# Attention with a learned position bias and a feed-forward layer: the short query chunk first, two chunks with f32 exponentials transposed on TensorE, the weights' integer steps through PSUM

## The chip, the cores and the metric

The kernel runs on one core of a Trainium2 chip. The metric is the device time of one execution in microseconds (us); the time of the kernel before is the median of three runs. The engines are named as in the profile: PE is TensorE's matmul stream and PEld its weight loads, DVE is VectorE, ACT is ScalarE, POOL is GpSimd, and SP is SyncE, which issues all DMAs of this kernel.

## The reference, cut to what matters

```python
# q, k, v: (4, 8, 576, 64) f32; w1 (1, 32), b1 (32), w2 (32, 8)
scores = scale * np.matmul(q, k.transpose(0, 1, 3, 2))
x = (np.log1p(np.abs(i - j)) / np.log1p(np.maximum(i, 1.0)))[..., None]
bias = np.maximum(x @ w1 + b1, 0.0) @ w2          # (576, 576, 8), one plane a head
scores = scores + bias.transpose(2, 0, 1)[None]
attn = np.exp(scores - np.max(scores, axis=-1, keepdims=True))
attn = attn / (np.sum(attn, axis=-1, keepdims=True) + 1e-09)
y = np.matmul(attn, v)                            # heads side by side: (2304, 512)
h = np.maximum(y @ w_in, 0.0)                     # w_in (512, 2048) float64
out = (h * h @ w_out).astype(np.float32)          # w_out (2048, 512) float64
```

## The kernel before

**Tiling.** The four batches are taken as two pairs (p = 0, 1). A pair's 576 queries are cut into five chunks: c = 1 to 4 hold 128 queries of both batches, c = 0 holds the last 64 queries of both batches side by side on the 128 partitions. One step is (p, c, head), so there are 80 steps, eight to a chunk. In a step with c = 1 to 4 (a full step) the softmax works on two rows of 576 per partition, one for each batch; in a step of c = 0 (a short step) on one. `ORDER` sets the chunks of p = 0 to 3, 0, 2, 4, 1 and those of p = 1 to 1, 0, 4, 2, 3.

**A step.** `qk` multiplies q and k, both split into a high and a low f16 part, into the PSUM tile `sc` (there is one). `softmax_a` adds the bias tile `bt` and takes the row maximum on DVE (L367), forms the negated maximum (L370), and takes the exponential with its sum on ACT (L373). `softmax_b` splits the exponentials into f16 parts: ACT casts (tile `a`, L118 by way of `cast`), POOL subtracts (L384, L385), and a DMA transposes the two parts to `at` (L387). `pv`, called three steps later (`LAG`), multiplies `at` with the split `v` in 28 f16 matmuls of 64 columns (L411). After a chunk's last head `finish_x` scales the chunk, splits it (`xh`, L448 and L449) and transposes it by DMA to `xt`.

**The feed-forward layer.** A finished chunk gives eight units: `g1` (24 matmuls into `hp`, L465, then ACT, DVE and POOL make the squared and split `g`) and, three units later, `g2` (12 matmuls into `o0` and `o1` for a full chunk, 6 into `o0` for the short one, L488). One unit goes with each step, two when more than ten are waiting (`BACKLOG`).

**Weights.** They arrive as float64 in 32 tiles of 128 x 512 values through the staging tiles `stg` (three, shared with k and v). `WT.split` makes f32 of each by three integer instructions on DVE in the SBUF tile `cv` (L185, L186, L188), casts the high part on ACT (`ENG["wh"]`), scales `cv` in place on ACT (`ENG["wl"]`, POOL for the last tiles) and subtracts on POOL (L203). `W_AT` says how many of the 32 tiles are loaded in each of the first 32 steps; they lie between step 4 and step 30.

**Bias.** For 16 query positions and all heads at once, a group, `hgen` makes four hidden tiles `hg` on DVE (L266) or ACT (L263; the string `HID` has the number on ACT for each pair of groups), and `bias_mm` multiplies them in f32 into `bp` (L293), evacuates `be` (L304) and writes it to a table in DRAM (L308); `bias_ld` reads the step's `bt` back. `bias_due` sets how many of the 36 groups are done after each step; ten are done ahead of step 0.

**Order.** A scheduler places the instructions of each engine by priority and by its own estimate of time, so that engines do not follow the source's order strictly; on each engine the built order is then fixed. The PSUM tiles of `bp` and `hp` share two buffers (`ps_h`).

## Time and profile before

| | us |
|---|---|
| median of three runs | 705.91 (705.66 to 707.59) |
| the profiled execution | 710.13 |
| span of its instructions | 708.4 |
| PE busy | 611.1 |
| DVE busy | 453.9 |
| POOL busy | 385.4 |
| ACT busy | 357.3 |

The span runs from the first instruction to the last; the profiled execution took 1.7 us more than its span. Busy times are unions over the whole span, and the engines work in stages with different limits, so the table alone does not tell which engine sets the time: the stages do, and they are read from the rows further below.

### The profile page before, as it was taken

How to read it: one execution, taken by the hardware profiler on the slowest of the kernel's cores; microseconds unless marked ns; L12 is line 12 of the kernel's file. 1: busy time of each engine (PE TensorE's matmuls, PEld its weight loads, DVE VectorE, ACT ScalarE, POOL GpSimd, SP SyncE). 2: the span in 40 equal slices, each digit the busy share in tenths (PEclk: the TensorE clock that was granted, in tenths of full speed). 3: DMA queues.
4: the chain of work that ended last, by engine and by line, in shares of the span. 5: the costliest groups of instructions: out<-in, count | busy, mean ns of one | idle time of the engine just before them, and what ended most of it. 6: DMA issues, size and time to landing. Idle time of an engine off the chain costs nothing.

```text
span 708.4 us, 15644 instructions
## 1 busy us (share of the span) xinstructions
PE 611.1 (86%) x6056; PEld 377.9 (53%) x6056; DVE 453.9 (64%) x977; ACT 357.3 (50%) x710; POOL 385.4 (54%) x375
## 2 busy tenths in 40 slices
...
GB/s 217 213 239 279 225 235 259 233 258 196 194 240 143 175 227 165 158 185 162 211 237 128 174 168 150 84 143 114 141 153 205 190 156 155 95 131 31 25 7 30
DMA packets 235881, 119.25 MB, mean 168 GB/s; under 512 B 196384, under 2 KB 212768, under 8 KB 235808
## 3 DMA queue, kind: packets, MB, share of 16 engines
...
## 4 chain that ended last, share of the span: by engine, by line
PE 52%; DVE 18%; DMA 14%; issue 6%; ACT 5%; POOL 4%; SPq 0%; DVEq 0%; POOLq 0%; ACTq 0%
PE hp L465 20%; PE o L488 19%; DMA at<-a 7%; PE pv L411 5%; PE sc L352 3%; PE bp L293 3%; DVE hg L266 3%; DVE cv L186 3%; POOL a L385 2%; DVE s L367 2%; DVE cv L188 2%; DVE cv L185 2%; DMA biasd<-be 1%; ACT s L373 1%; ACT a L118 1%
## 5 line engine op out<-in xcount | busy, mean ns | idle before, releaser
L465 PE MATMUL hp<-xt,winH 128*128 128x256 f16 (+1 forms) x1280 | 202.4, 268 | 15.3 <-DVE r L473 14.0
L488 PE MATMUL o<-woutH,g 128*128 128x512 f16 x576 | 184.4, 380 | 0.9 <-ACT o L495 0.9
L373 ACT ACTIVATE s<-s,nm 128x576 f32<-128x576 f32 x144 | 110.5, 768 | 136.6 <-DVE nm L370 136.1
L465 PE MATMUL hp<-xt,winL 128*128 128x256 f16 (+1 forms) x640 | 165.7, 267 | 0.3 <-POOL winL L203 0.3
L385 POOL TENSOR_TENSOR a<-s,a 128x1024 f16<-128x1024 f32 (+1 forms) x80 | 162.6, 2033 | 0.0
L465 PEld LDWEIGHTS <-winH 128*128 128x128 f16 x1280 | 118.7, 100 | 51.3 <-issue 20.1
L367 DVE CUSTOM_DVE_ANT_0 s<-sc,bt 128x576 f32<-128x576 f32 x144 | 103.4, 750 | 45.3 <-PE sc L352 23.3
L488 PEld LDWEIGHTS <-g 128*128 128x128 f16 x864 | 82.8, 98 | 90.4 <-issue 6.7
L473 DVE TENSOR_TENSOR r<-hp,r 128x512 f32<-128x512 f32 (+1 forms) x80 | 50.6, 633 | 117.0 <-ACT r L471 116.6
L475 POOL TENSOR_TENSOR g<-r,g 128x512 f16<-128x512 f32 (+1 forms) x80 | 86.8, 1085 | 66.8 <-DVE g L122 64.4
L411 PEld LDWEIGHTS <-at 128*128 128x128 f16 (+1 forms) x2240 | 80.6, 105 | 71.3 <-DMA at<-a 38.7
L384 POOL TENSOR_TENSOR a<-s,a 128x128 f16<-128x128 f32 (+1 forms) x80 | 37.0, 463 | 146.5 <-ACT a L118 118.5
L411 PE MATMUL pv<-v,at 128*128 128x64 f16 (+1 forms) x2240 | 88.8, 199 | 30.7 <-DMA at<-a 28.9
L118 ACT ACTIVATE a<-s 128x1152 f16<-128x1152 f32 (+1 forms) x80 | 85.1, 1064 | 49.9 <-DMA at<-a 48.9
L488 PE MATMUL o<-woutL,g 128*128 128x512 f16 x288 | 109.4, 380 | 0.0
L471 ACT ACTIVATE r<-hp 128x512 f32<-128x512 f32 (+1 forms) x80 | 43.2, 540 | 64.9 <-PE hp L465 64.3
L266 DVE TENSOR_SCALAR hg<-tab_t,nb 128x352 f32<-128x352 f32 (+17 forms) x102 | 67.1, 708 | 13.1 <-PE bp L293 11.4
L293 PE MATMUL bp<-hg,w2s 128*32 128x288 f32 (+17 forms) x352 | 62.0, 550 | 14.8 <-ACT be L304 10.4
L465 PEld LDWEIGHTS <-winL 128*128 128x128 f16 x640 | 64.0, 100 | 8.2 <-issue 0.8
L352 PE MATMUL sc<-k,q 64*128 64x512 f16 x384 | 57.0, 398 | 0.0
L304 ACT ACTIVATE be<-bp,hcst 128x288 f32<-128x288 f32 (+32 forms) x80 | 34.5, 473 | 20.8 <-PE bp L293 14.4
L122 DVE TENSOR_SCALAR g<-r 128x512 f16<-128x512 f32 (+1 forms) x61 | 40.0, 656 | 2.1
...
## 6 DMA issues: line engine op xcount, KB each, us to landing
...
```

The costliest lines, as they stand in the source:

```text
L118: nc.scalar.activation(out=out, in_=in_, func=AF.Copy, scale=scale)
L266: nc.vector.tensor_scalar(ht, tab_t[:, 0:dlen(G)], scl[:, n:n + 1], nb1, op0=ALU.mult, op1=ALU.max)
L293: nc.tensor.matmul(out=bp[32 * t:32 * t + 32, 0:d1 - d0], lhsT=w2s, rhs=ts_[t][:, d0:d1], start=True, stop=True, tile_position=(0, 32 * t))
L352: nc.tensor.matmul(out=sc[:, 1024 * b:1024 * b + 512], lhsT=qt[r, qz, qs], rhs=kt[r, z, 64 * b:64 * b + 512], start=(n == 0), stop=(n == 2 ...
L367: nc.vector.tensor_tensor_reduce(s[:, 576 * b:576 * b + 576], sc[:, 960 * b:960 * b + 576], bt, inv, -3.0e38, ALU.add, ALU.max, mx[:, b:b ...
L373: nc.scalar.activation(out=sl, in_=sl, func=AF.Exp, bias=nm[:, b:b + 1], accum_out=su[:, h, b:b + 1])
L385: nc.gpsimd.tensor_tensor(av[:, :, 640:1152], ev[:, :, 0:512], av[:, :, 0:512], op=ALU.subtract)
L411: nc.tensor.matmul(out=dst, lhsT=lhsT, rhs=vt[:, vz, 5 * b + blk, :], start=(n == 0), stop=(n == 13), tile_position=(0, 0 if c else 64 * b))
L465: nc.tensor.matmul(out=hp[:, f * T:f * T + T].rearrange("p (b t) -> p b t", b=nb), lhsT=wt[:, k, c0:c0 + 128], rhs=xt[:, 0:nb, z * 4 + k, ...
L473: nc.vector.tensor_tensor(rr, hp[:, 0:2 * T], rr, op=ALU.mult)
L475: nc.gpsimd.tensor_tensor(g[:, 1, 0:2 * T], r[:, 0:2 * T], g[:, 0, 0:2 * T], op=ALU.subtract)
L488: nc.tensor.matmul(out=blk["o"][b], lhsT=g[:, z, c0:c0 + 128], rhs=wt[:, 2 * u + f, :], start=(u == 0 and f == 0 and z == 0 and wt is wout ...
```

## The change

- **Order of the chunks.** p = 0 begins with the short chunk: 0, 3, 2, 4, 1. The order of p = 1 stays.
- **Two chunks in f32** (`NF = 2`: the first two, so c = 0 and c = 3 of p = 0). Their exponentials are not split and not sent through a DMA. In `softmax_b` TensorE transposes them in f32 against an identity (five 128-column transposes in a short step, ten in a full one) into tiles `tp` of the pool `ps_h`, and ACT copies these to `at` (two copies in a short step, three in a full one). `pv` multiplies with the unsplit v in ten f32 matmuls.
- **v of p = 0** lands by DMA directly in the tiles of the pool `vp` (nine now) and is split only in steps 16 to 23.
- **Weights.** The first two integer steps write the PSUM tile `ci`, which takes the buffer of `o1`; the third reads it and writes `cv`. All high parts are cast on ACT, all scalings go to POOL. All 32 tiles are loaded in the first 16 steps.
- **Bias.** Four groups are done ahead of step 0, since the short chunk needs four, and `HID` puts 34 hidden tiles on ACT instead of 42.
- **Buffers.** `qst` and `xh` have one buffer instead of two.

```diff
-    "wh": "AAPAAAAA", "wl": "AAAAAAAP", "qh": "PPPDDP",
+    "wh": "AAAAAAAA", "wl": "PPPPPPPP", "qh": "PPPDDP",
...
-HID = "110033320111212000"
+HID = "221111111111111000"
...
+W_AT = [1, 1, 2, 2, 2, 2, 2, 2, 3, 3, 3, 2, 2, 2, 2, 1] + [0] * 16
+ORDER = [[0, 3, 2, 4, 1], [1, 0, 4, 2, 3]]
+NF = 2
...
-    vp = pool("vp", 8)
+    vp = pool("vp", 9)
-    qst_p = pool("qst", 2)
+    qst_p = pool("qst", 1)
-    xh_p = pool("xh", 2)
+    xh_p = pool("xh", 1)
...
+    f32c = [(0, c) for c in ORDER[0][:NF]]
+    def as_f32(t):
+        return t.rearrange("p a b -> p (a b)").bitcast(F32)
+    def v_split(p, h, st):
+        t = vp.tile([128, 2, 640], F16, tag="v", name="v")
+        cast(zn("vh", p * 8 + h), t[:, 0, :], st, float(2 ** VS))
+        nc.vector.scalar_tensor_tensor(
+            out=t[:, 1, :], in0=st, scalar=float(2 ** VS), in1=t[:, 0, :],
+            op0=ALU.mult, op1=ALU.subtract)
+        nc.gpsimd.memset(t[64:128, 1, :].rearrange("p (b j) -> p b j", b=2)[:, :, 256:320], 0.0)
+        v_t[p, h] = t
...
-            self.st = stg_p.tile([128, 1024], F32, tag="stg", name="stg")
+            if self.which == "v" and self.p == 0:
+                self.st = as_f32(vp.tile([128, 2, 640], F16, tag="v", name="v"))
+                v32[self.h] = self.st
+            else:
+                self.st = stg_p.tile([128, 1024], F32, tag="stg", name="stg")
...
-            ci = cv.bitcast(U32)
+            ci = ps_o.tile([128, 512], F32, tag="o1", name="ci").bitcast(U32)
             nc.vector.tensor_scalar(ci, hi32, 3, 0x3FFFFFFF, op0=ALU.logical_shift_left, op1=ALU.bitwise_and)
             nc.vector.scalar_tensor_tensor(out=ci, in0=lo32, scalar=29, in1=ci,
                                            op0=ALU.logical_shift_right, op1=ALU.bitwise_or)
-            nc.vector.scalar_tensor_tensor(out=ci, in0=hi32, scalar=0xC0000000, in1=ci,
+            nc.vector.scalar_tensor_tensor(out=cv.bitcast(U32), in0=hi32, scalar=0xC0000000, in1=ci,
                                            op0=ALU.bitwise_and, op1=ALU.bitwise_or)
...
     def softmax_b(p, c, h):
+        if (p, c) in f32c:
+            at = as_f32(at_p.tile([128, 20, 128], F16, tag="at", name="at")).rearrange("p (k i) -> p k i", i=128)
+            for b in range(nb):
+                tp = ps_h.tile([128, 512], F32, tag="h", name="tp")
+                for k in range(4):
+                    nc.tensor.transpose(tp[:, 128 * k:128 * k + 128], e[:, S * b + 128 * k:S * b + 128 * k + 128], ident)
+                nc.scalar.activation(out=at[:, 4 * b:4 * b + 4, :], in_=tp.rearrange("p (k i) -> p k i", i=128), func=AF.Copy)
+            tp = ps_h.tile([128, 512], F32, tag="h", name="tp")
+            for b in range(nb):
+                nc.tensor.transpose(tp[0:64, 128 * b:128 * b + 128], e[:, S * b + 512:S * b + 576], ident)
+            nc.scalar.activation(out=at[0:64, 4 * nb:5 * nb, :], in_=tp[0:64, 0:128 * nb].rearrange("p (k i) -> p k i", i=128),
+                                 func=AF.Copy)
+            st_[p, c, h, "t"] = at
+            return
...
     def pv(p, c, h):
+            if f32:
+                for blk in range(5):
+                    r = slice(0, 128 if blk < 4 else 64)
+                    if c:
+                        lhsT = at[r, 4 * b + blk if blk < 4 else 8 + b, :]
+                    else:
+                        lhsT = at[r, blk, 64 * b:64 * b + 64]
+                    nc.tensor.matmul(out=dst, lhsT=lhsT, rhs=vt[r, 5 * b + blk, :], start=(blk == 0), stop=(blk == 4),
+                                     tile_position=(0, 0 if c else 64 * b))
+                continue
...
     def bias_due(t):
-        k = (t + AHEAD) // H + 1
+        if t < 0:
+            return due[0]
+        ahead = min(AHEAD, t + 1)
+        k = (t + ahead) // H + 1
...
+        if NF * H <= t < NF * H + H:
+            v_split(0, t - NF * H, v32.pop(t - NF * H))
```

What this moves in the built program is shown at three places. On ACT, at the end of the first full chunk of the kernel before: `a<-s` is the f16 cast that feeds the transposing DMA, `cv<-cv` the scaling of a weight tile, `be<-bp` the evacuation of the bias.

```order
L373 ACTIVATE s,sum<-s,nm 128x576 x2
L118 ACTIVATE woutH<-cv 128x512
L304 ACTIVATE be<-bp,hcst 128x432
L304 ACTIVATE be<-bp,hcst 128x159
L118 ACTIVATE a<-s 128x2x576
L420 ACTIVATE rd<-sum,eps 128x8
L118 ACTIVATE cv<-cv 128x512
```

In the changed kernel, in steps 9 and 10, which belong to its first full chunk, ACT has this (`at<-tp` copies the transposed exponentials out of PSUM):

```order
L388 ACTIVATE s,sum<-s,nm 128x576
L401 ACTIVATE at<-tp 128x512
L388 ACTIVATE s,sum<-s,nm 128x576
L121 ACTIVATE woutH<-cv 128x512
L401 ACTIVATE at<-tp 128x512
L405 ACTIVATE at<-tp 64x256
L485 ACTIVATE os<-ax 128x1
L278 ACTIVATE hg<-tab_t,sm_t 128x384
```

The cast and the scaling are gone from ACT, and three copies per full step stand there, behind transposes on PE.

On DVE, in the same places of the two programs (the end of the first full chunk before; steps 8 to 10 now), the three integer steps of a weight tile:

```order
L185 TENSOR_SCALAR cv<-stg 128x512
L229 SCALAR_TENSOR_TENSOR q<-qst,q 128x512
L370 TENSOR_SCALAR nm<-mx 128x1
L266 TENSOR_SCALAR hg<-tab_t,nb_131 128x400 x2
L370 TENSOR_SCALAR nm<-mx 128x1
L186 SCALAR_TENSOR_TENSOR cv<-stg,cv 128x512
L185 TENSOR_SCALAR cv<-stg 128x512
L188 SCALAR_TENSOR_TENSOR cv<-stg,cv 128x512
```

```order
L281 TENSOR_SCALAR hg<-tab_t,nb_131 128x400
L200 TENSOR_SCALAR ci<-stg 128x512
L281 TENSOR_SCALAR hg<-tab_t,nb_131 128x400 x2
L385 TENSOR_SCALAR nm<-mx 128x1
L201 SCALAR_TENSOR_TENSOR ci<-stg,ci 128x512
L464 TENSOR_TENSOR x<-pv,rd 128x256
L203 SCALAR_TENSOR_TENSOR cv<-stg,ci 128x512
L481 TENSOR_REDUCE ax<-x 128x1
```

The number of instructions per tile is the same; the second operand and, for two of the three, the output lie in PSUM. All 32 tiles now stand ahead of step 16's maximum; before, 22 did and the last ten stood ahead of step 24's.

On PE, the bias group of 496 columns in the last bias chunk (c = 1, steps 24 to 31 in both programs). Before, each of its four matmuls stands alone among those of `g1` or `pv`:

```order
L465 LDWEIGHTS winL
L465 MATMUL hp<-xt,winL 128x128
L465 LDWEIGHTS winH
L465 MATMUL hp<-xt,winH 128x128
L293 MATMUL bp<-hg,w2s 32x496
```

```order
L452 LDWEIGHTS at
L452 MATMUL pv<-v,at 128x64
L308 MATMUL bp<-hg,w2s 32x496 x3
L506 LDWEIGHTS winH
L506 MATMUL hp<-xt,winH 128x256
```

Three of the four now follow each other directly; the groups of 512, 480 and 464 columns, which were split up before too, have all four together.

## Rows read from the trace of the kernel before

**Rows 1.** The busy time of each engine in us, with its number of instructions, then the granted TensorE clock as a share of 2.4 GHz, the DMA share and GB/s, in six stretches (start:end and length come first; the engines follow as PE, PEld, DVE, ACT, POOL). They are cut where DVE starts the first maximum (L367) of steps 0, 8, 16, 24 and 32.

```profile
0.00:32.40 32.40, 20.96 (x129) 6.37 (x130) 23.87 (x61) 21.22 (x44) 12.10 (x22) 0.96 0.68 204
32.40:90.90 58.50, 27.80 (x277) 12.61 (x277) 49.90 (x92) 43.41 (x86) 37.39 (x34) 0.67 0.96 252
90.90:159.70 68.80, 42.26 (x421) 25.25 (x421) 60.72 (x106) 38.48 (x78) 42.45 (x42) 0.78 1.00 245
159.70:235.60 75.90, 63.18 (x589) 35.07 (x591) 65.59 (x119) 47.64 (x94) 55.36 (x48) 0.87 0.81 192
235.60:301.10 65.50, 61.31 (x645) 33.52 (x641) 44.61 (x103) 36.85 (x77) 33.66 (x34) 1.00 0.85 183
301.10:708.40 407.30, 395.61 (x4003) 265.08 (x4001) 209.25 (x503) 169.69 (x336) 204.47 (x197) 1.00 0.65 134
```

**Rows 2.** The chain of work that ended last, after 525 us: start, length, engine, tile, line, number of instructions.

```profile
526.73 1.45 PE hp L465 x24
528.18 1.29 PE o L488 x6
...
548.81 4.94 DMA xt<-xh
...
625.92 1.63 PE pv L411 x56
627.55 2.62 PE hp L465 x24
630.17 2.59 PE o L488 x12
```

**Rows 3.** Who waited for whom from 90 to 236 us: us in total, times, longest.

```profile
PE sc L340 <- DVE mx L367: 16.0, 3, 7.6
...
ACT woutH L118 <- DVE cv L188: 13.7, 7, 5.4
```

**Rows 4.** Groups of instructions on DVE over the whole span: us busy, mean ns of one, idle time before. L188, L186 and L185 are the integer steps of the 32 weight tiles.

```profile
L188 DVE SCALAR_TENSOR_TENSOR cv<-stg,cv 128x512 uint32<-128x512 uint32 x32 | 34.0, 1068 | 0.4
L186 DVE SCALAR_TENSOR_TENSOR cv<-stg,cv 128x512 uint32<-128x512 uint32 x32 | 31.7, 1000 | 0.3
L185 DVE TENSOR_SCALAR cv<-stg 128x512 uint32<-128x512 uint32 x32 | 22.6, 712 | 5.4 <-DMA stg<-w_in 4.6 <-DMA stg<-w_out 0.9
...
L229 DVE SCALAR_TENSOR_TENSOR q<-qst,q 128x512 f16<-128x512 f32 x20 | 17.0, 852 | 9.0 <-POOL q L120 9.0
...
L146 DVE SCALAR_TENSOR_TENSOR k<-stg,k 128x576 f16<-128x576 f32 x14 | 11.6, 830 | 11.4 <-POOL k L120 11.4
```

**Rows 5.** DVE instructions of single lines over the whole span: number, duration in ns as minimum/median/maximum, first and last start, shapes. L473 reads one operand from PSUM and one from SBUF; L186 and L188 read both from SBUF.

```profile
L186 DVE SCALAR_TENSOR_TENSOR cv<-stg,cv x32: 654/750/2548, 43.3 to 214.1; 128x512 uint32<-128x512 uint32 x32
...
L188 DVE SCALAR_TENSOR_TENSOR cv<-stg,cv x32: 634/692/2619, 45.2 to 216.4; 128x512 uint32<-128x512 uint32 x32
...
L473 DVE TENSOR_TENSOR r<-hp,r x80: 407/691/693, 135.4 to 695.0; 128x512 f32<-128x512 f32 x64, 128x256 f32<-128x256 f32 x16
...
L266 DVE TENSOR_SCALAR hg<-tab_t,nb x102: 420/540/2381, 4.6 to 283.4; 128x368 f32<-128x368 f32 x8, 128x384 f32<-128x384 f32 x8, 128x336 f32<-128x336 f32 x7, 128x352 f32<-128x352 f32 x7
...
L367 DVE CUSTOM_DVE_ANT_0 s<-sc,bt x144: 700/752/759, 32.4 to 621.4; 128x576 f32<-128x576 f32 x144
...
L157 DVE SCALAR_TENSOR_TENSOR v<-stg,v x16: 808/1126/2737, 14.8 to 383.0; 128x640 f16<-128x640 f32 x16
```

**Rows 6.** Groups of instructions on POOL up to 160 us, shapes kept apart, columns as in rows 4.

```profile
L385 POOL TENSOR_TENSOR a<-s,a 128x1024 f16<-128x1024 f32 x8 | 19.1, 2387 | 0.0
L203 POOL TENSOR_TENSOR woutL<-cv,woutH 128x512 f16<-128x512 f32 x10 | 13.1, 1321 | 0.1
```

**Rows 7.** Who waited for whom from 235 to 301 us, columns as in rows 3.

```profile
PE pv L411 <- DMA at<-a: 3.8, 2, 2.0
```

**Rows 8.** The chain in the same stretch, columns as in rows 2.

```profile
242.37 7.05 DMA at<-a
```

**Rows 9.** The chain up to 34 us.

```profile
24.51 4.14 DMA biasd<-be
...
28.74 3.63 DMA bt<-biasd
```

**Rows 10.** Groups on ACT over the whole span, shapes kept apart: the evacuation of 288 columns of bias out of PSUM, and a hidden tile of 544 columns.

```profile
L304 ACT ACTIVATE be<-bp,hcst 128x288 f32<-128x288 f32 x7 | 3.4, 492 | 1.6 <-PE bp L293 1.6
...
L263 ACT ACTIVATE hg<-tab_t,sm_t 128x544 f32<-128x544 f32 x3 | 2.4, 833 | 0.0
```

**Rows 11.** PE in order of time; the profile has two records for an f32 matmul. A bias group of 512 columns whose four matmuls stand together, the first and the last of the four of 496 columns that stand alone, and the score matmuls of a full step.

```profile
224.38 1.94 PE L293 MATMUL bp<-hg,w2s 128*32 128x512 f32 x8
...
269.26 1.02 PE L293 MATMUL bp<-hg,w2s 128*32 128x496 f32 x2
...
273.75 1.02 PE L293 MATMUL bp<-hg,w2s 128*32 128x496 f32 x2
...
276.30 0.33 PE L346 MATMUL sc<-kz,q 128*128 128x128 f16 x3
...
286.70 0.82 PE L352 MATMUL sc<-k,q 64*128 64x512 f16 x6
```

**Rows 12.** Weight loads in order of time: 14 f16 loads of 128 columns, and the two of one f32 matmul with 32 columns.

```profile
253.32 0.50 PEld L411 LDWEIGHTS <-at 128*128 128x128 f16 x14
...
254.04 0.14 PEld L293 LDWEIGHTS bp<-hg,w2s 128*32 128x32 f32 x2
```

More of the change, by code (lines that the diff above doesn't have):

```diff
@@ L106, in tile_attention_moe @@
     eps = const.tile([128, 1], F32, name="eps")
+    ident = const.tile([128, 128], F32, name="ident")
     sc = ps_sc.tile([128, 1536], F32, name="sc")
@@ L152, in split @@
                 k_t[self.p, self.h] = t
-            else:
-                t = vp.tile([128, 2, 640], F16, tag="v", name="v")
-                st = st[:, 0:640]
-                cast(zn("vh", self.p * 8 + self.h), t[:, 0, :], st, float(2 ** VS))
-                nc.vector.scalar_tensor_tensor(
-                    out=t[:, 1, :], in0=st, scalar=float(2 ** VS), in1=t[:, 0, :],
-                    op0=ALU.mult, op1=ALU.subtract)
-                nc.gpsimd.memset(t[64:128, 1, :].rearrange("p (b j) -> p b j", b=2)[:, :, 256:320], 0.0)
-                v_t[self.p, self.h] = t
+            elif self.p:
+                v_split(self.p, self.h, st[:, 0:640])
     class WT:
@@ L255, in hgen @@
                 elif pl == "at":
-                    h2 = at_p.tile([128, 18, 128], F16, tag="at", name="hg").rearrange("p k i -> p (k i)").bitcast(F32)
+                    h2 = at_p.tile([128, 20, 128], F16, tag="at", name="hg").rearrange("p k i -> p (k i)").bitcast(F32)
                 elif pl == "s":
@@ L385, in softmax_b @@
         nc.gpsimd.tensor_tensor(av[:, :, 640:1152], ev[:, :, 0:512], av[:, :, 0:512], op=ALU.subtract)
-        at = at_p.tile([128, 18, 128], F16, tag="at", name="at")
+        at = at_p.tile([128, 20, 128], F16, tag="at", name="at")
         nc.sync.dma_start_transpose(out=at[:, 0:9 * nb, :], in_=a[:, 0:nb * 2 * S])
@@ L394, in pv @@
         at = st_.pop((p, c, h, "t"))
-        vt = v_t[p, h].rearrange("p z (j d) -> p z j d", d=D)
+        f32 = (p, c) in f32c
+        vt = v32[h].rearrange("p (j d) -> p j d", d=D) if f32 else v_t[p, h].rearrange("p z (j d) -> p z j d", d=D)
         if h % 4 == 0:
```

11 lines of the change are left out of this document (6 added, 5 removed).

## The prediction

> **What bounds the kernel now.** I read the stretches first, cut where steps 0, 8, 16, 24 and 32 begin [rows 1]. In the last one, 301.1 to 708.4 us, PE is busy for 395.61 of 407.30 us at a granted clock of 1.00, its 2.4 GHz level, and the chain there is PE, unit after unit: 24 matmuls in 2.62 us, 12 in 2.59 us [rows 2]. That part is PE's own work, and nothing ahead of it can shorten it. So the question is only when step 32 begins, how much of PE's work is done by then, and whether the later part gets new waits.
>
> Ahead of it PE is not the limit: busy 27.80 of 58.50 us, 42.26 of 68.80, 63.18 of 75.90, at mean clocks of 0.67 to 0.87, that is, partly at the 1.2 GHz level. DVE is busy for 49.90, 60.72 and 65.59 us of these stretches, 85 to 88% [rows 1], and others wait for it: PE's scores for the maximum, 16.0 us, ACT's weight casts for the last integer step, 13.7 us [rows 3]. DVE's largest item there is the weights: 34.0 + 31.7 + 22.6 = 88.3 us for 32 tiles, 2.78 us each [rows 4]. Their medians are 0.69 and 0.75 us, but single ones take over 2.5 us [rows 5], about as long as POOL's subtraction of 1024 elements, 2387 ns [rows 6]. An instruction of the same length with one operand in PSUM, L473, has a median of 691 and a maximum of 693 ns: it is never held up [rows 5]. I take it that POOL's subtraction holds up DVE instructions that use SBUF twice.
>
> In the fifth stretch, 235.6 to 301.1 us, the weights are gone and DVE is busy for only 44.61 us [rows 1]. What costs there is transposing DMAs on the chain, one of 7.05 us [rows 8], for which PE waits 3.8 us in all [rows 7], and bias matmuls of which below.
>
> **The change part by part.** The sum is made on the span, 708.4 us. The profiled execution took 710.13 us, 1.7 us more, and is itself 4.2 us above the median of 705.91; I work out the shift of the span and set it against the median.
>
> *PE's work left at step 32* is the same. Counting DVE's `r` instructions of the units in the two built programs gives 19 units ahead of step 32 in both: 8 of the short chunk, 8 of c = 3, and 3 of c = 2. All bias is done soon after in both. So the last stretch stays 407.3 us.
>
> *Start.* Four bias groups stand ahead of step 0, not ten. They need 8 hidden tiles on ACT at 0.83 us (6.7 us) and 12 evacuations near 0.49 us (5.9 us) [rows 10], with a weight cast and key copies between them in ACT's order; then, as now, the write (4.14 us) and the read (3.63 us) of the table [rows 9]. Step 0 then starts at about 29 us instead of 32.4; 27 at best, and no gain at worst.
>
> *Steps 0 to 15.* They took 58.5 + 68.8 = 127.3 us, with DVE busy for 110.6. I change DVE's load by what the built programs count between the same steps. Weights: 22 tiles go, which cost 22 x 0.712 + 43 x 1.034 = 60.1 us, and 31.3 come. At L473's 0.69 us a step, 2.07 a tile, that is 64.8 us. An integer step that writes PSUM is in no row: the lower end is the minimum of the SBUF forms, 0.65 us, the upper end the present 2.78 us a tile. I take L473, which has the same size and one PSUM operand; the gain a tile, 0.71 us, is the hold-ups. Hidden tiles: 51 on DVE instead of 27, 24 x 0.54 = 13.0 us. One more k and one more v cost 0.83 + 1.13 us; one split of `xh` fewer saves 1.6 by the length of a q split, 0.85, twice. Sum: +18 us. Against it stands that POOL has no subtractions of exponentials in these 16 steps, 2.4 us each in a full one, but more weight subtractions of 1.3 us [rows 6]. So hidden tiles and v should be near their medians (0.54 and 1.13 us) rather than held for up to 2.4 us, and the ends of neighbouring DVE instructions overlap; I take 7 us off, between 0 and 12. DVE's load is then 122 us (117 to 129), and at the share of now, 110.6/127.3 = 0.87, the 16 steps take 140 us (134 to 148), 13 more than now. Step 16 starts at 169 us instead of 159.7.
>
> *PE in these steps.* Per full step 28 f16 matmuls of 29 ns go (56 in 1.63 us [rows 2]), and 10 f32 matmuls and 10 transposes come. The rows have f32 matmuls with 32 stationary columns only. By them an f32 matmul has two records and costs 1.9 us/2/512, 1.9 ns a column, where four on different columns of the array share it [rows 11]: 0.12 us for 64 columns. Its loads follow each other by 0.03 us for 32 columns, as do f16 loads of 128 [rows 12]. With 128 f32 columns a load takes between 0.03 and 0.12 us, so a matmul between 0.12 and 0.24 us, a transpose between 0.06 (one record) and 0.24. I take 0.24 and 0.16, 4.0 us a full step (1.8 to 4.8) and some 2 us a short one. In steps 8 to 15 PE then has 8 x (4.0 + 1.0 for the scores [rows 11]), 5 us of bias and about 7 us of half units (1.45 + 1.29 us each [rows 2]): 52 us at 2.4 GHz, against some 84 us of DVE. It lies beside DVE's work. The Trainium skill, "TensorE: Matmul & The Clock Gate", section on weight-path perf modes, says that the fast weight load is not used for f32; that speaks for the upper end of a load, and no row here has an f32 load of 128 columns.
>
> *ACT* loses 28 scalings and 16 casts and gains 40 copies of PSUM, each like an evacuation of bias; it was busy 43.41 of 58.5 us at most and stays below DVE. *POOL* loses 16 subtractions and gains 28 scalings; it stays below too. *SP* loses 16 transposing DMAs. Its `qst` loads, with one buffer, wait for the split of the last q, and bias and score loads queue behind them; a q is used for four steps, so I cost this at nothing; uncovered it would be one q split, 0.85 us, each time.
>
> *Steps 16 to 23.* Now 75.9 us with ten weight tiles and DVE at 65.59. After the change DVE's list there is that of the fifth stretch, 44.61 us, which took 65.5 us. That stretch also lost PE time to bias matmuls that stand alone: a group costs 1.94 us/2 together, but 4 x 1.02 us alone [rows 11]. In the changed order the four stand together or 3 and 1, which spares about 6 us in all over four groups. So I take 60 us for steps 16 to 23 (56 to 66), and 63 us for steps 24 to 31 (60 to 66), where two thirds of the units are full ones and PE is the limit: 8 x (5.2 + 1.0 + 0.8) = 56 us and 8 of bias, less half units.
>
> *Later.* With one `xh` buffer the second transposing DMA of a block waits for the first. It shows where no unit is left, as at 548.81 us, 4.94 us on the chain [rows 2]; +3 us (0 to 5).
>
> *Sum.* 29 + 140 + 60 + 63 = 292 us for the start of step 32, where it was 301.1; 292 + 407.3 + 3 = 702.3 us of span, 6.1 below 708.4. Against the median: 705.9 - 6.1 = 700 us.
>
> **The rivals.** *PE is the limit of steps 8 to 15 (slower).* The transposes wait for ACT, the matmuls for ACT's copies, and the next scores stand behind both in PE's fixed order. If PE stays at 1.2 GHz there, its 52 us become 104 against 84 of DVE, and with 16 matmuls f32 at the same rate in the short steps a few more: +20 to +25, 720 us or more. It decides where the mean clock falls below 52/84 = 0.62. The stretch now with PE busy 48% has 0.67, that with 61% has 0.78 [rows 1], which speaks against it; the waits within PE's order speak for it. The Trainium skill has a rule for this side too, in the same page's "PE-mode transpose": it says that the full clock does not engage for transposes. By that the time would be this rival's; the rows have no transposes on PE, and the trace cannot show it.
>
> *The PSUM form is no faster.* At 2.78 us a tile DVE has 31 x 0.71 = 22 us more, 25 us of time: 724 us. For it speaks only that no row has an integer step on PSUM.
>
> *It comes out even.* Each full f32 step passes exponential, transposes, copies and matmuls through two `ps_h` buffers shared with bias and units. Another 0.8 us a full step that DVE spends waiting gives the gain back: 706 us.
>
> *More is released.* If hidden tiles, v and k fall to their minima (0.42, 0.81 us) and the integer steps to 0.65, DVE has 115 us; at 0.88 that is 130, and steps 16 to 23 at 56: 292 - 14 = 278, 686 us.
>
> **How the numbers follow.** About 0.3%, 2.1 us, is what a measurement of this kernel tells from no change, so faster ends at 703.8 and slower begins at 708.0. Forecast, 692 to 703.8: 0.38. More released, 676 to 692: 0.20. Even, 703.8 to 708: 0.16. PE the limit, 708 to 735: 0.20; the PSUM form, 708 to 726: 0.06. So faster 0.58, same 0.16, slower 0.26. The range of 8 in 10 leaves out the lower third of "more" and half of the two slow ones: 681 to 718.
>
> **What would show it.** Right: L201 and L203 with maxima near 0.7 us; step 0 near 29, step 16 near 169, step 24 near 229, step 32 near 292 us; 407 us from there to the end, and PE above 95% busy in them; DVE the busiest engine up to step 16. Wrong: a granted clock below 0.62 in steps 8 to 15 with PE busy throughout (PE the limit); integer steps above 0.9 us (the PSUM form); DVE's share below 0.8 in steps 8 to 15 with PE or ACT waiting on each other (even); step 16 before 160 us (more released). The sum as a whole is wrong if the stretch after step 32 differs from 407 us by more than 5.

## The result, and the profile after

The changed kernel takes 713.04 us (median of 4 runs, 711.86 to 716.15), the kernel before 705.79; the ratio is 1.0104, 95% interval 1.0068 to 1.0139. It is **slower by 1.0%** where the forecast was 0.8% faster. The time lies inside the stated range, on the other side.

The profiled execution took 713.13 us, its span is 711.2. The stretches of the profile after, cut at the first maximum (L382) of steps 0, 8, 16, 24 and 32, columns as in [rows 1]:

```profile
0.00:34.00 34.00, 11.47 (x78) 2.65 (x78) 15.65 (x39) 14.85 (x30) 11.15 (x21) 1.00 0.77 243
34.00:94.20 60.20, 44.74 (x306) 24.21 (x306) 48.32 (x96) 35.94 (x82) 22.94 (x27) 0.77 0.69 208
94.20:175.00 80.80, 65.71 (x436) 43.73 (x436) 73.47 (x151) 46.99 (x104) 48.32 (x61) 0.77 0.67 198
175.00:231.80 56.80, 53.67 (x572) 32.74 (x572) 45.94 (x99) 41.19 (x85) 31.75 (x34) 1.00 0.78 166
231.80:301.70 69.90, 67.42 (x652) 40.09 (x651) 43.70 (x99) 32.84 (x67) 34.87 (x34) 0.98 0.71 155
301.70:711.20 409.50, 396.18 (x4011) 265.03 (x4009) 210.21 (x502) 170.45 (x337) 203.38 (x197) 1.00 0.65 134
```

| us | before [rows 1] | forecast | after | error |
|---|---|---|---|---|
| start | 32.4 | 29 | 34.0 | +5.0 |
| steps 0 to 15 | 127.3 | 140 | 141.0 | +1.0 |
| steps 16 to 23 | 75.9 | 60 | 56.8 | -3.2 |
| steps 24 to 31 | 65.5 | 63 | 69.9 | +6.9 |
| from step 32 on | 407.3 | 410.3 | 409.5 | -0.8 |
| span | 708.4 | 702.3 | 711.2 | +8.9 |

The forecast of the time was 700 us, so 13 us are missing: 8.9 in this table, and the other 4 are the reference, since the profile before was of an execution 4.2 us above its median and the profile after is at its median.

The weights' integer steps after (number, shortest/median/longest in ns, first and last start), against [rows 4, 5]:

```profile
L200 DVE TENSOR_SCALAR ci<-stg x32: 676/694/717, 12.9 to 169.1; 128x512 uint32<-128x512 uint32 x32
L201 DVE SCALAR_TENSOR_TENSOR ci<-stg,ci x32: 677/695/699, 14.8 to 171.9; 128x512 uint32<-128x512 uint32 x32
L203 DVE SCALAR_TENSOR_TENSOR cv<-stg,ci x32: 670/680/689, 22.0 to 172.7; 128x512 uint32<-128x512 uint32 x32
```

None is held up: 2.07 us a tile, as forecast, for 2.78. DVE's load up to step 16 is 48.32 + 73.47 = 121.8 us (forecast: 122).

**The start.** SP's issues in order of time (start, length, line, number), and then two waits up to 34 us (us, times, longest):

```profile
5.27 1.57 SPq L156 DMA_DIRECT2D v<-vd  x3
...
8.44 3.06 SPq L156 DMA_DIRECT2D v<-vd  x4
...
13.67 1.69 SPq L323 DMA_DIRECT2D biasd<-be  x2
...
24.56 1.33 SPq L323 DMA_DIRECT2D biasd<-be  x3
30.29 1.12 SPq L336 DMA_DIRECT2D bt<-biasd  x2
```

```profile
DVE s L382 <- DMA bt<-biasd: 9.8, 1, 9.8
...
ACT be L319 <- DMA biasd<-be: 4.9, 3, 4.1
```

The first bias was evacuated by 11.2 us and its write is issued at 13.67, behind eight loads of v (the first of them at 2.18 us) and two of q at 12.03. ACT then waits 4.9 us for `be` buffers whose writes have not landed. The last write and the read that step 0 waits for take from 24.56 to 34.0 us, against 7.8 us for the two DMAs of [rows 9].

**Steps 24 to 31.** The units' matmuls with `winH` there (number, shortest/median/longest in ns; all are 256 columns wide, so there are full units only), then the chain (start, length):

```profile
L506 PE MATMUL hp<-xt,winH x130: 272/273/421, 234.1 to 301.6; 128*128 128x256 f16 x130
```

```profile
275.81 4.10 DMA xt<-xh
...
279.96 4.41 PE hp L506 x24
```

PE stands still for 2.5 us until the second transposing DMA of the block lands, and the unit behind it takes 4.41 us where [rows 2] have 2.62. The granted clock falls behind the stand: it is 0.74 from 280 to 282 us and 0.51 from 282 to 284.4 us.

### The profile page after: what moved, and what is told of

Its sections match the earlier page's. It is cut to its first block, busy times and chain, and to the rows that moved or that the text cites. A ratio compares the mean times of both kernels' runs of the same rounds, so it can differ in the third digit from the quotient of the medians.

```text
span 711.2 us, 15582 instructions
## 1 busy us (share of the span) xinstructions
PE 639.2 (90%) x6048; PEld 408.5 (57%) x6048; DVE 437.3 (61%) x981; ACT 342.3 (48%) x702; POOL 352.4 (50%) x369
## 4 chain that ended last, share of the span: by engine, by line
PE 48%; DVE 12%; DMA 8%; issue 5%; POOL 3%; ACT 3%; SPq 0%; ACTq 0%; POOLq 0%; DVEq 0%
PE hp L506 18%; PE o L529 18%; DMA at<-a 6%; PE pv L452 4%; PE sc L367 3%; DVE s L382 2%; DVE hg L281 2%; DMA xt<-xh 2%; PE bp L308 2%; POOL a L415 1%; DVE r L514 1%; ACT a L121 1%; DVE xh L490 1%; DVE xh L489 1%; PE sc L355 1%
## 5 line engine op out<-in xcount | busy, mean ns | idle before, releaser
L506 PE MATMUL hp<-xt,winH 128*128 128x256 f16 (+1 forms) x1280 | 198.7, 265 | 3.5 <-DMA xt<-xh 3.1
L382 DVE CUSTOM_DVE_ANT_0 s<-sc,bt 128x576 f32<-128x576 f32 x144 | 103.5, 750 | 52.9 <-PE sc L367 28.0
L415 POOL TENSOR_TENSOR a<-s,a 128x1024 f16<-128x1024 f32 (+1 forms) x64 | 130.4, 2037 | 0.0
L516 POOL TENSOR_TENSOR g<-r,g 128x512 f16<-128x512 f32 (+1 forms) x80 | 85.3, 1066 | 73.4 <-DVE g L125 70.5
L414 POOL TENSOR_TENSOR a<-s,a 128x128 f16<-128x128 f32 (+1 forms) x64 | 28.4, 443 | 133.7 <-ACT a L121 117.7
L121 ACT ACTIVATE a<-s 128x1152 f16<-128x1152 f32 (+1 forms) x64 | 70.4, 1101 | 43.0 <-DMA at<-a 42.2
L281 DVE TENSOR_SCALAR hg<-tab_t,nb 128x464 f32<-128x464 f32 (+17 forms) x110 | 68.1, 673 | 10.2 <-PE bp L308 9.9
L452 PEld LDWEIGHTS <-at 128*128 128x128 f16 (+1 forms) x1792 | 60.3, 100 | 23.6 <-issue 8.1
L452 PE MATMUL pv<-v,at 128*128 128x64 f16 (+1 forms) x1792 | 64.2, 194 | 3.5 <-DMA at<-a 3.5
L308 PE MATMUL bp<-hg,w2s 128*32 128x288 f32 (+17 forms) x352 | 50.1, 574 | 13.2 <-ACT be L319 6.6
L367 PE MATMUL sc<-k,q 64*128 64x512 f16 x384 | 55.1, 395 | 0.0
L445 PEld LDWEIGHTS pv<-v,at 128*64 128x64 f32 (+3 forms) x320 | 40.8, 201 | 20.6 <-issue 11.7
L123 POOL TENSOR_SCALAR cv<-cv 128x512 f32<-128x512 f32 x32 | 21.4, 668 | 55.7 <-ACT winH L121 34.5
```

Source lines behind the costliest of these rows:

```text
L121: nc.scalar.activation(out=out, in_=in_, func=AF.Copy, scale=scale)
L281: nc.vector.tensor_scalar(ht, tab_t[:, 0:dlen(G)], scl[:, n:n + 1], nb1, op0=ALU.mult, op1=ALU.max)
L308: nc.tensor.matmul(out=bp[32 * t:32 * t + 32, 0:d1 - d0], lhsT=w2s, rhs=ts_[t][:, d0:d1], start=True, stop=True, tile_position=(0, 32 * t))
L367: nc.tensor.matmul(out=sc[:, 1024 * b:1024 * b + 512], lhsT=qt[r, qz, qs], rhs=kt[r, z, 64 * b:64 * b + 512], start=(n == 0), stop=(n == 2 ...
L382: nc.vector.tensor_tensor_reduce(s[:, 576 * b:576 * b + 576], sc[:, 960 * b:960 * b + 576], bt, inv, -3.0e38, ALU.add, ALU.max, mx[:, b:b ...
L415: nc.gpsimd.tensor_tensor(av[:, :, 640:1152], ev[:, :, 0:512], av[:, :, 0:512], op=ALU.subtract)
```

## The experiments

Each gives the median time, the ratio to the kernel before with its interval, and its stretches cut as above. The planner orders every build anew, so a stretch that an edit doesn't touch can move too. The runs come from several sessions. The kernel before was run in each, with medians from 705.8 to 709.5 us; the changed kernel was run in the first alone, so a difference to it in us is uncertain by up to some 4 us, and the ratios are the better comparison.

| run | us | ratio (95%) | start | 0-7 | 8-15 | 16-23 | 24-31 | rest |
|---|---|---|---|---|---|---|---|---|
| after | 713.0 | 1.0104 (1.0068-1.0139) | 34.0 | 60.2 | 80.8 | 56.8 | 69.9 | 409.5 |
| e1_before_again | 707.7 | one run | 32.5 | 59.0 | 68.6 | 74.8 | 66.3 | 404.8 |
| e2_ci_sbuf | 720.5 | 1.0182 (1.0158-1.0205) | 32.8 | 70.1 | 80.6 | 56.2 | 67.4 | 411.2 |
| e3_xh_r | 697.8 | 0.9863 (0.9841-0.9884) | 32.0 | 61.5 | 74.1 | 57.4 | 66.5 | 406.2 |
| e4_v_late | 705.0 | 0.9966 (0.9937-0.9994) | 30.8 | 62.8 | 73.8 | 56.5 | 67.6 | 409.1 |
| e5_nf1 | 719.5 | 1.0149 (1.0109-1.0188) | 33.6 | 66.5 | 86.3 | 52.2 | 69.4 | 411.9 |
| e6_no_lo | 697.8 | 0.9858 (0.9812-0.9905) | 33.7 | 59.9 | 67.2 | 56.1 | 67.7 | 409.5 |
| e7_xh_r5 | 707.8 | 1.0002 (0.9978-1.0026) | 33.9 | 61.2 | 78.4 | 56.8 | 70.6 | 406.2 |
| e8_xh_v | 698.6 | 0.9870 (0.9834-0.9905) | 30.0 | 64.5 | 73.6 | 57.1 | 66.6 | 407.3 |
| e9_tp_o0 | 698.7 | 0.9884 (0.9826-0.9941) | 35.9 | 49.6 | 73.6 | 56.6 | 70.4 | 410.4 |
| e10_xh_hid | 701.0 | 0.9909 (0.9878-0.9940) | 31.0 | 63.9 | 73.9 | 58.2 | 67.3 | 406.6 |
| e11_xh_wat | 697.8 | 0.9861 (0.9797-0.9926) | 31.3 | 64.7 | 67.7 | 56.4 | 66.2 | 408.3 |
| e12_xh_tp_wat | 694.7 | see there | 34.3 | 53.9 | 75.9 | 56.6 | 66.6 | 403.7 |
| e13_nf0 | 715.5 | 1.0087 (1.0057-1.0118) | 31.6 | 69.3 | 77.4 | 59.6 | 66.3 | 409.6 |
| e14_xh_tp_wat_v | 695.0 | 0.9787 (0.9749-0.9824) | 30.5 | 56.7 | 71.3 | 56.3 | 66.7 | 407.2 |
| e15_pv2 | 752.4 | 1.0623 (1.0575-1.0671) | 33.1 | 63.4 | 109.3 | 65.5 | 70.5 | 413.9 |

**The kernel before once more** (e1_before_again).

> The kernel before, unchanged, to have a second profile of it. The profile that the prediction rests on is of an execution of 710.13 us, 4.2 above the median. Theory: an execution near the median, 705.7 us, has a span near 704, and its missing 4 us lie ahead of step 32, where the engines wait for each other; the stretch after step 32 is 407 us again, give or take 1. Rival: they lie in PE's own stretch after step 32 (403 us).

The span is 706.0 us, 2.4 less. The rival holds: 2.5 us lie behind step 32, and step 32 begins at 301.2 us, as in [rows 1]. Single executions of the same build lay between 705.57 and 711.75 us beside it. So PE's own stretch is not a constant to better than some 3 us, and one profile does not fix the zero of a sum.

**The integer steps back in SBUF** (e2_ci_sbuf).

```diff
-            ci = ps_o.tile([128, 512], F32, tag="o1", name="ci").bitcast(U32)
+            ci = cv.bitcast(U32)
```

> The changed kernel with the integer steps back in the SBUF tile cv. Theory (POOL's subtractions hold up DVE instructions that use SBUF twice, and DVE is the bound up to step 16): an integer tile costs 2.78 us again instead of 2.07, 31 x 0.71 = 22 us of DVE, 25 us of time, 735 to 740 us. Rival 1: POOL has no subtractions of exponentials there, only 1.15 us of weights, so the hold-ups are half: 720 to 727 us. Rival 2: no hold-ups or another engine is the bound: 711 to 716 us.

The three steps there, on DVE over the span (us, mean ns):

```profile
L201 DVE SCALAR_TENSOR_TENSOR cv<-stg,cv 128x512 uint32<-128x512 uint32 x32 | 26.7, 853 | 0.1
L203 DVE SCALAR_TENSOR_TENSOR cv<-stg,cv 128x512 uint32<-128x512 uint32 x32 | 26.2, 834 | 0.2
...
L200 DVE TENSOR_SCALAR cv<-stg 128x512 uint32<-128x512 uint32 x32 | 17.7, 577 | 1.5 <-DMA stg<-w_in 1.5
```

7.5 us slower (5.5 by the two ratios), at the edge of rival 1. Steps 0 to 7 are 9.9 us longer, steps 8 to 15 the same. A tile costs 0.853 + 0.834 + 0.577 = 2.26 us, not 2.78: with POOL's 2.4 us subtractions of exponentials [rows 6] gone from these steps, most of the hold-up is gone without PSUM. The two traces bear this out. In the kernel before, each of the 24 integer steps longer than 1.2 us lies beside a subtraction of two tensors on POOL, and the four above 2 us lie beside L385 with 2.25 to 2.58 us. Here there are eleven, all beside subtractions of weights, and none is above 1.67 us. PSUM frees the two-operand steps (853 and 834 to 691 and 681) and slows the first, 577 to 692, all in the mean.

**The second xh** (e3_xh_r, e7_xh_r5). The tiles come from the ring of `r`, with six buffers in the first run, five in the second.

```diff
-    r_p = pool("r", 5)
+    r_p = pool("r", 6)
...
-            xh = xh_p.tile([128, 1024], F16, tag="xh", name="xh")
+            xh = r_p.tile([128, 512], F32, tag="r", name="xh").bitcast(F16)
```

> The changed kernel with the xh tiles taken from the ring of r, which gets a sixth buffer, so that two splits of a block are in flight again with the same memory. Theory: at 277.5 us PE stood idle for 2.5 us for the transposing DMA and then took 4.40 us for a unit instead of 2.75, 4.1 us in all, since the second split waited for the first one's DMA; these go, and up to 3 us later: 706 to 709 us. Rival: the wait is DVE's list ahead of the split (hidden tiles of 3.7 us), not the buffer: 712 to 714 us.

> As the run with xh from the ring of r (697.8 us), but that ring keeps five buffers; the 2 KB of xh are left unused. It tells the second xh apart from the sixth buffer, which the bias evacuations and the weights' cv also use. Theory: the second split in flight gives steps 24 to 31 in 66 to 67 us and about 4 us, the sixth buffer the rest, which came in the start and in steps 8 to 15: 706 to 710 us. Rival: the order that the planner makes is what moved steps 8 to 15, not the sixth buffer: any time from 697 to 703 us.

Steps 24 to 31 of e3_xh_r, without the wait, and a wait in the same steps of e7_xh_r5:

```profile
225.00:291.50 66.50, 65.83 (x653) 39.20 (x652) 44.97 (x99) 33.19 (x69) 34.06 (x33) 1.00 0.74 161
```

```profile
PE bp L308 <- ACT be L319: 3.4, 1, 3.4
```

The wait for `xt` is gone in both runs. Behind step 32 the second `xh` gives 3.3 us with either ring, and the runs with one `xh` took 409.1 to 413.9 us there, those with two 403.7 to 408.3. In steps 24 to 31 the 3.4 us come with six buffers only; with five the wait for `xt` gives way to one for a bias evacuation. The two runs differ in the ring alone, apart from the order, so the sixth buffer is worth 10.0 us (707.75 to 697.76): 1.9 in the start, 4.3 in steps 8 to 15, 4.1 in steps 24 to 31. The 15 us of e3_xh_r were more than forecast; 6.7 came in steps 8 to 15.

What the single `xh` costs in steps 24 to 31 hangs on the clock. In e2_ci_sbuf, e4_v_late, e6_no_lo and e13_nf0 PE waits 1.6 to 1.9 us for `xt`, no matmul of a unit takes over 283 ns, and the stretch is 66.3 to 67.7 us, little above e3_xh_r. In the changed kernel, e5_nf1, e9_tp_o0 and e15_pv2 it waits 2.0 to 2.8 us, matmuls of 421 ns follow, and the stretch is 69.4 to 70.5 us.

**Six loads of v later** (e4_v_late, e8_xh_v).

```diff
                 v32[self.h] = self.st
+                if last_nm:
+                    nc.gpsimd.tensor_scalar(self.st[:, 0:1], last_nm[0], 1.0, 1.0, op0=ALU.mult, op1=ALU.mult)
...
         st_[p, c, h] = s
+        last_nm[:] = [nm[:, 0:1]]
```

> The changed kernel with the loads of v of heads 2 to 7 held back until a step's maximum is negated. Theory: step 0 begins at 34.0 us since the bias writes stand on SP's queue behind 8 loads of v and 4 of weights; six loads of 320 KB at some 243 GB/s are 8 us of transfers, so step 0 begins at 28 to 30 us and the whole takes 707 to 710 us. Rival 1: the weights' loads alone fill the queue, step 0 at 33 to 34 us and 712 to 714 us. Rival 2: step 0 is earlier, but DVE's list up to step 16 is as long as before and sets its end: 712 to 714 us.

> Both edits, xh from the ring of r with six buffers and six loads of v held back. Theory: the start of the second (30.8 us) and the later stretches of the first add up: 694 to 697 us. Rival: both had gained the same 7 us in steps 8 to 15, and the start is only another 1 us: 697 to 700 us.

Step 0 begins at 30.8 us alone, at 30.0 with the `xh` edit: 2.0 to 3.2 us of the start are the loads of v. e4_v_late is below its forecast of 707 to 710 us, since 7.0 us came in steps 8 to 15. SP's issues in its start show a second cause of late writes:

```profile
11.08 1.27 SPq L238 DMA_DIRECT2D qst<-qd  x2
12.40 1.07 SPq L326 DMA_DIRECT2D biasd<-be  x2
```

SP has waited 2.7 us there until DVE has split the first q out of the single `qst`. The first two evacuations had ended by 11.1 us, and their writes go out 1.3 us later, behind these loads. No run has a second `qst`, so what that wait costs step 0 is not shown. Added to the second `xh` they bring no more time (698.6 against 697.8), since steps 0 to 7 take 3 us more: the rival holds.

**One chunk in f32, and none** (e5_nf1, e13_nf0).

```diff
-NF = 2
+NF = 1
```

> The changed kernel with only the short chunk in f32 (NF = 1); the exponentials of c = 3 are split again, cast on ACT, subtracted on POOL (2.4 us a step) and transposed by DMA, and v is split in steps 8 to 15. Theory (DVE is the bound up to step 16, the f32 path lies beside it and keeps POOL's long subtractions away): 16 us more of POOL's subtractions hold DVE up again and the v splits stay, so steps 8 to 15 take 2 to 8 us longer, 715 to 721 us. Rival: PE's transposes, f32 matmuls and their waits at the lower clock limit these steps; without them they get 5 to 10 us shorter: 703 to 708 us.

> The changed kernel with no chunk in f32 (NF = 0); v of p = 0 is loaded through the staging tiles and split at once, as in the kernel before; the weights' integer steps stay in PSUM. Theory (in the short chunk the f32 path cost about 10 us through the two shared PSUM buffers, in c = 3 it gained 6): steps 0 to 7 lose the transposes and copies but get 8 v splits of some 1.1 us on DVE and 8 more loads through the staging tiles, 56 to 60 us; steps 8 to 15 as with c = 3 in f16 less the v splits, 76 to 80 us: 706 to 714 us in all. Rival: the f32 path is a gain in both chunks: 720 us or more.

Of e5_nf1 the total came as the theory had it, and steps 8 to 15 got 5.5 us longer; steps 0 to 7, which it didn't name, 6.3. In e13_nf0, where v goes through the staging tiles again too, steps 0 to 7 take 69.3 us, not 56 to 60, and the start and steps 8 to 15 and 24 to 31 give most of it back. 715.5 and 713.0 are not told apart, their intervals overlap: the f32 path as built, with its loads of v, is worth about nothing in all.

**Without the second integer step** (e6_no_lo; the weights' lowest three bits are left out).

```diff
-            nc.vector.scalar_tensor_tensor(out=ci, in0=lo32, scalar=29, in1=ci,
-                                           op0=ALU.logical_shift_right, op1=ALU.bitwise_or)
```

> The changed kernel without the second integer step, so the weights' lowest three mantissa bits (those from the low word) are left out; DVE does 32 x 0.69 = 22 us less up to step 16. Theory (DVE is the bound there): the 16 steps take 121 to 126 us instead of 141, 691 to 698 us. Rival (PE at its lower clock, ACT and the waits within PE's order are as late as DVE): 5 us or less, 708 us or more.

697.8 us is at the upper end of the theory; the 127.1 us for the 16 steps lie just above its 121 to 126. Of the 13.9 us, 13.6 come from steps 8 to 15; steps 0 to 7 stay at 59.9 with DVE busy for only 43.56. DVE's load does not bind steps 0 to 7. It counts in steps 8 to 15, but how much of the 13.6 us is its own is not shown: some 7 us came there in e3_xh_r, e4_v_late and e9_tp_o0 too, which leave the integer steps alone.

**The short chunk's transposes in o0** (e9_tp_o0).

```diff
+            tpl = (ps_h, "h") if c else (ps_o, "o0")
             for b in range(nb):
-                tp = ps_h.tile([128, 512], F32, tag="h", name="tp")
+                tp = tpl[0].tile([128, 512], F32, tag=tpl[1], name="tp")
```

> The changed kernel with the short chunk's transposes written to the PSUM tile o0, which is free until the first unit, instead of the two buffers shared with bias. In the run without the second integer step DVE had 5 us less work in steps 0 to 7 and the stretch stayed at 59.9 us, so DVE is not its bound. Theory: PE, ACT's copies and evacuations wait for each other through the two buffers; with a third place steps 0 to 7 take 52 to 56 us instead of 60.2: 705 to 709 us. Rival: loads and ACT's order set these steps: 58 us or more, 711 to 714 us.

Two of PE's waits in steps 0 to 7 of the changed kernel (us, times, longest), then the same steps of e9_tp_o0:

```profile
PE bp L308 <- ACT at L401: 2.9, 5, 1.2
PE tp L404 <- ACT be L319: 2.5, 2, 1.5
```

```profile
35.90:85.50 49.60, 37.77 (x285) 21.00 (x283) 43.56 (x90) 32.55 (x74) 23.11 (x26) 0.90 0.85 254
```

Bias waits for ACT's copies of transposes and transposes for evacuations of bias, in turns. With a third place the 8 steps lose 10.6 us, twice the 5.4 of the two waits. The start takes 1.9 us more and has more of their work in it (DVE busy for 22.35 us of it, not 15.65), so step 8 begins 8.7 us earlier. Another 7.2 us came in steps 8 to 15, which the edit does not touch. The granted clock of steps 0 to 7 goes from 0.77 to 0.90; with two levels, 2 x (1 - clock) x length estimates 27.7 us at the 1.2 GHz level against 9.9. The Trainium skill, "TensorE: Matmul & The Clock Gate", section "A second HAM failure mode: psum-queue depth-cycling", tells of a kernel whose cycling through PSUM let PE idle so often that its clock went up and down. These two traces agree with it, 0.77 against 0.90.

**More hidden tiles on ACT; weights spread evenly** (e10_xh_hid, e11_xh_wat, both on e3_xh_r).

```diff
-HID = "221111111111111000"
+HID = "222222222222111000"
```

```diff
-W_AT = [1, 1, 2, 2, 2, 2, 2, 2, 3, 3, 3, 2, 2, 2, 2, 1] + [0] * 16
+W_AT = [2] * 16 + [0] * 16
```

> As the run with xh from the ring of r and six buffers (697.8 us), with 54 hidden tiles on ACT instead of 34: 8 of them in steps 0 to 7, 8 in steps 8 to 15, 4 behind. Theory: DVE is the bound of steps 8 to 15 alone (busy 71.8 of 74.1 us in that run), 8 x 0.60 = 4.8 us go there: 68 to 70 us, and 692 to 694 us in all. Rival: the evacuations behind these tiles on ACT come later and PE's bias matmuls with them, 697 us or more.

> As the run with xh from the ring of r and six buffers (697.8 us), with two weight tiles loaded in each of the first 16 steps instead of 14 in the first eight and 18 in the next. Theory: DVE has 10 us of idle time in steps 0 to 7 and none in steps 8 to 15; two tiles of 2.07 us moved ahead shorten the latter by 4 us and lengthen the former by less than 2: 694 to 696 us. Rival: the three staging tiles, not the list of loads, set when a tile is taken, nothing moves: 697 to 699 us.

Neither came as its theory had it. With the tiles on ACT, DVE has 5.1 us less in steps 8 to 15 and they stay at 73.9 us; 701.0 us is the rival's. With the weights even they go from 74.1 to 67.7, and steps 0 to 7 from 61.5 to 64.7; in all nothing, 697.8. DVE alone does not set these steps.

**Three edits, four edits** (e12_xh_tp_wat: e3_xh_r, e9_tp_o0 and e11_xh_wat together; e14_xh_tp_wat_v: e4_v_late as well).

> Three edits together: xh from the ring of r with six buffers, the short chunk's transposes in o0, two weight tiles in each of the first 16 steps. Theory: each takes away a wait of its own stretch, so the shortest of each add up: start 33 us, steps 0 to 7 50 to 52, steps 8 to 15 68 to 72, steps 16 to 23 56.5, steps 24 to 31 66.4, then 406.5: 681 to 685 of span, 683 to 687 us. Rival: the better stretches after step 8 were one and the same gain in each run, and the start eats the weights moved ahead: 690 to 697 us.

> As the run with the three edits together, and six loads of v held back until a step's maximum is negated. Theory: the start is bound by SP's queue and what it moves, and goes from some 33 to 35 us to 30 to 31: 3 to 4 us less than that run. Rival: with o0 for the transposes steps 0 to 7 wait for the loads of k, weights and v instead (in the run with o0 PE waited 4.1 and 2.8 us for casts of k), and the v loads now stand among them: no gain, or 1 to 3 us more.

The gains add up in part. The eight executions of the three edits go from 685.32 to 702.66 us, too far apart for an interval, so I give the ratio of the medians, 694.71/709.50 = 0.979; it lies in the rival's range. The four edits, in six runs from 690.45 to 697.83, are 0.9787 (0.9749 to 0.9824): faster than the kernel before by 2.1%, and than the changed one by 1 - 0.9787/1.0104 = 3.1%, by way of the two ratios. Their start is 30.5 against 34.3 us, as the theory of the queue had it, but steps 0 to 7 give 2.8 of it back, and the totals are the same, as its rival had it.

Steps 8 to 15 of e11_xh_wat, e14_xh_tp_wat_v and e12_xh_tp_wat:

```profile
96.00:163.70 67.70, 56.86 (x438) 38.17 (x439) 65.59 (x142) 44.19 (x100) 41.47 (x53) 0.86 0.70 205
```

```profile
87.20:158.50 71.30, 59.47 (x432) 41.12 (x431) 65.66 (x138) 42.74 (x98) 42.30 (x52) 0.82 0.68 201
```

```profile
88.20:164.10 75.90, 63.52 (x440) 43.62 (x441) 65.65 (x140) 44.75 (x98) 44.67 (x54) 0.74 0.66 192
```

The same 65.6 us of DVE lie in 67.7, 71.3 and 75.9 us; what differs with the length is the clock, 0.86, 0.82, 0.74. Which of the two follows from the other these profiles do not show. The next run changes PE's work alone.

**The f32 matmuls of c = 3 twice** (e15_pv2).

```diff
-                for blk in range(5):
+                for blk in (0, 1, 2, 3, 4) * (2 if c else 1):
```

> The changed kernel with the ten f32 matmuls of a full step of c = 3 issued twice (the second pass begins its sums anew, the result is the same). A matmul was 0.18 us in the records, so it adds 8 x 1.8 = 14 us to PE, in steps 11 to 18, at the mean clock there, some 11 of them up to step 16. Theory (PE is the limit in the stretches at the 1.2 GHz level, DVE in those at 2.4 GHz): of steps 8 to 15, 37 of 81 us were at the lower level, so they get some 5 us longer, and 3 in the steps behind, where PE is the limit as well: 718 to 724 us. Rival 1 (DVE alone is the bound of steps 8 to 15, PE's work lies beside it): only the 3 us behind: 714 to 717 us. Rival 2: the more PE has to do, the longer its clock stays at the upper level, which gives the time back: 713 us or less.

Its steps 8 to 15 and 16 to 23, then three pieces of 6 us:

```profile
96.50:205.80 109.30, 95.96 (x549) 70.51 (x550) 72.66 (x149) 47.14 (x104) 48.04 (x60) 0.64 0.48 145
205.80:271.30 65.50, 60.49 (x618) 38.88 (x617) 44.86 (x99) 40.54 (x83) 32.44 (x35) 0.95 0.68 141
```

```profile
130.00:136.00 6.00, 6.00 (x27) 4.21 (x27) 1.63 (x4) 0.00 (x0) 0.37 (x1) 0.50 0.55 171
...
166.00:172.00 6.00, 6.00 (x28) 3.90 (x24) 1.13 (x3) 0.00 (x0) 1.08 (x2) 0.50 0.06 23
172.00:178.00 6.00, 0.17 (x4) 0.00 (x0) 5.86 (x10) 2.26 (x5) 3.55 (x5) 0.50 0.33 89
```

39 us more, above every forecast; and the clock of steps 8 to 15 went down, from 0.77 to 0.64, where rival 2 had it stay up. PE's matmuls of a step, in order of time in the changed kernel, tell why: the ten of `pv` (20 records) and transposes, at the 1.2 GHz level (107 to 114 us) and at 2.4 GHz (161 to 166 us):

```profile
107.76 3.20 PE L445 MATMUL pv<-v,at 64*128 64x64 f32 x12
...
112.72 1.12 PE L400 MATMUL tp<-ident,s 128*128 128x128 f32 x4
113.63 1.81 PE L445 MATMUL pv<-v,at 128*128 128x64 f32 x8
...
161.56 1.73 PE L445 MATMUL pv<-v,at 64*128 64x64 f32 x12
163.22 1.09 PE L400 MATMUL tp<-ident,s 128*128 128x128 f32 x8
...
165.80 1.00 PE L445 MATMUL pv<-v,at 128*128 128x64 f32 x8
```

A step's `pv` takes 5.0 us at the lower level and 2.73 at the upper. Five of them lie in steps 8 to 15, 5 x 5.0 = 25 us, and the steps got 28.5 longer; three lie behind, 3 x 2.73 = 8.2, and those got 8.7 longer. Nothing of it was hidden. The other 7 us of the 44.5 by which the span grew lie in stretches that the edit does not touch, 4.4 of them behind step 32.

## Why the prediction was wrong

Of the 13 us, 5.0 are the start, 6.9 steps 24 to 31 and 4.2 the zero of the sum; steps 16 to 23 gave 3.2 back. The first two turned a gain into a loss.

**Start, failed.** "Step 0 then starts at about 29 us ... and no gain at worst": 34.0. The working priced ACT's tiles and evacuations and took the two DMAs as before. It did not price what the direct landing of v puts ahead of them on SP's queue: with nothing to wait for, all eight loads go first. Shown: 30.8 us with six of them held back, 30.5 against 34.3 in the kernel with the three other edits. It put the wait for the single `qst` at nothing; in e4_v_late it holds the first writes up by 1.3 us. How the last 2 us to the forecast divide stays open.

**Steps 24 to 31, mis-sized.** The 63 us took two thirds of the units for full ones; all are, and without any wait for `xt` the stretch is 66.5 us with PE busy 65.83. The other 3.4 are the single `xh`, which was priced at 3 us and placed behind step 32 alone: a stand of 2.5 us and a unit at the lower clock behind it. That the clock fell is particular to some builds; the others with one `xh` lost 1 us or so. Behind step 32 it is 3.3 (409.5 against 406.2), as said.

**Steps 0 to 15, the number right and half of its reason wrong.** DVE's load, 121.8 us, and 141.0 us came as forecast. That the time did is in part luck: the share of 0.87 stands for 0.80 in steps 0 to 7, with the waits at `ps_h`, and 0.91 in steps 8 to 15. "It lies beside DVE's work", of PE, failed, and so did the test of the rival on it, "where the mean clock falls below 52/84 = 0.62". The 84 us of DVE in it were 73.5, so it should have been 0.71, which 0.77 passes as well; but the mean hides two regimes. Pieces of the changed kernel's steps 8 to 15:

```profile
106.00:110.00 4.00, 4.00 (x22) 2.90 (x22) 4.00 (x14) 2.97 (x7) 1.28 (x2) 0.61 0.67 202
110.00:114.00 4.00, 4.00 (x20) 2.45 (x19) 2.49 (x5) 0.86 (x4) 1.76 (x3) 0.50 0.44 133
...
118.00:122.00 4.00, 4.00 (x19) 3.06 (x21) 2.10 (x9) 3.32 (x8) 0.73 (x1) 0.50 0.62 143
130.00:134.00 4.00, 3.89 (x18) 2.48 (x18) 3.96 (x12) 2.44 (x7) 1.66 (x2) 0.50 0.78 229
146.00:150.00 4.00, 1.69 (x12) 0.94 (x12) 3.97 (x7) 1.66 (x4) 2.77 (x4) 1.00 0.42 132
166.00:170.00 4.00, 4.00 (x49) 3.18 (x47) 4.00 (x11) 2.29 (x6) 3.63 (x5) 1.00 0.98 277
```

From 110 to 114 and 118 to 122 us PE is busy throughout at 0.50 and DVE for 2.1 to 2.5 of 4 us: PE is the limit. From 146 to 150 us, at 1.00, DVE is, 3.97 of 4. Others have both full, at either level. Of the twenty pieces from 94 to 174 us DVE is below 3.6 us in five; these are granted 0.50 to 0.55, and PE is busy for 3.5 to 4.0 us in them. DVE stands still for 7.3 us in all here, so with its list as it is PE's limit has cost at most that. The mean clock, 0.77, decides nothing; by it 2 x 0.23 x 80.8 = 37 us were at the lower level. DVE's load (e6_no_lo) and PE's (e15_pv2) both count, each in its own pieces, and a load moved off DVE in e10_xh_hid bought nothing. The rival with the two `ps_h` buffers was right in kind, but it priced full steps: with a third place for the short ones step 8 begins 8.7 us earlier in e9_tp_o0.

PE's price itself was right: 2.73 + 10 x 0.136 = 4.1 us a full step at the upper clock, for the 4.0 taken.

**Steps 16 to 23, right**, 56.8 us for 60; the integer steps and DVE's load, right.

**The gain of PSUM, mis-sized.** The 0.71 us a tile of hold-ups was taken from a kernel in which POOL's long subtractions ran beside. In the changed one the same form without PSUM costs 2.26 us, not the 2.78 of the upper end. The two parts of the change remove the same hold-up; it can be gained once. The sum is not touched by this, since it took 2.07 us a tile, which came; only the rival's 724 us was too long.

**The zero.** The shift of the span, +2.8 us, was set against a median; between medians it is +7.25. Executions of the kernel before differ by up to 6 us in one session, and the range had no term for it.

Open: why steps 8 to 15 lost some 7 us in e3_xh_r, e4_v_late and e9_tp_o0 alike. DVE's idle time there is 7.3 us in the changed kernel and 2.3 in e3_xh_r, and 3.9 of the former were waits of the v splits for POOL (seven of the eight are placed ahead of step 16, not in steps 16 to 23); no run varied that alone. Of the 6.7 us in e3_xh_r, 4.3 came with the sixth buffer of `r`.
